# The second pass of Q and K by seven products of halves, x reloaded for the router, and a score bound from sums of squares

## The chip, the cores and the metric

The kernel runs on one core of one Trainium2 chip. The metric is the device time of one launch in microseconds; of several runs the median is given. TensorE (PE) multiplies, VectorE (DVE) and ScalarE (ACT) do elementwise work, GpSimd (POOL) a little of it, and DMA queues move data between memory and the core; SP, ACT and POOL each issue DMAs on a queue of their own.

## The reference

A gate g mixes two branches over one sequence of S = 2048 tokens with D = 1024 features. Branch a is attention with 32 heads of 32. Branch b is a router that picks, for each token and head, one of 8 x 8 experts, with the scores of two small key tables.

```python
g = sigmoid((x * gate_w).sum(-1, keepdims=True))
a = attention(x, wqkv) @ wo                    # H = 32, Dh = 32
b = router(x, w_q, k1, k2, u, v)               # E = 8, top 1, 32 heads, dk = 128
return g * a + (1 - g) * b
# router: q = x @ w_q; s1 = q1 . k1; s2 = q2 . k2; the best of each gives an expert;
# act = gelu(x . u[expert]); out = sum over heads of act * v[expert]
```

All inputs are float32, normal with a spread of 0.05.

## The kernel before

**Matrix products.** A float32 product is made of three fp32r products: each operand is split into a high part (`hi`, a rounding copy on ACT) and a low part (`lo`, source minus high part on DVE; `split`, L100), and high by high, high by low and low by high are summed in one PSUM bank. There are eight banks of 128 x 512.

**Q and K** are made transposed: 8 chunks of 128 rows each for Q and for K (two chunks `(w, c)` for each c; w is 0 for Q, 1 for K), and 4 token blocks n of 512. x lies in SBUF as split blocks `x_blk[n, ki]`, ki being the half of the features; only four places (names `xh0` to `xl3`) of that size exist beside scratch, so two passes are made.

**First pass**, token blocks 2 and 3. Chunk 0 is made while x comes in (L420), chunk 1 by four plain blocks of 24 matmuls (L514). Chunks 2 to 7 are six *units* (`qk_unit`, L519): Q and K of one chunk number by the two token blocks by the two halves of features is a 2 x 2 by 2 x 2 block product, and it is made by seven products P1 to P7 of 12 matmuls (`Halves.product`, L156) in place of eight. The left operands A11, A12, A22 and S1 to S4 are weights or sums of weights; the right ones are blocks of x or the sums T1 to T4 of blocks, made once for a pass. Each unit makes the next unit's left operands, and puts its products together on DVE (`u2`, `u3`, `u5`, `c1`; `tt`, L162; the copy of P1 is ACT's, L532). `hooks` names further work after a product of a unit.

**Second pass**, token blocks 0 and 1: 32 plain blocks of 24 matmuls (L734), in the order of `chunks`, weights split into two places (`pairs`) ahead (`w_chunk`). `between[b]` names further work after block b:

- `folds`: 32 times w_q is folded with the keys into the router's weights, 8 matmuls each (`fold`, L332) into a bank; every fourth fold ends with ACT's copy of the bank (`wt`), four transposes on PE (`fold_t`, L353), a copy and a store to DRAM (`WPD`) on POOL's queue;
- `gate`: DVE multiplies blocks of x by the gate's column and adds them up (`zacc`, L665); the high and low parts of each block are taken one after the other; `gate_sums` (L680) sums over partitions on PE;
- blocks of x are loaded again and split (`again`): (3,0) and (2,1), so that all four token blocks lie split in SBUF when the router starts;
- `load_wp`, `split_wp`: the router's weights, 8 pieces of 128 x 448 (the folded part, from DRAM, into six buffers `wpr`) and 128 x 64 (`ugr`), are loaded and split beside the last four blocks (`between[28]` to `[31]`).

Every block of Q and K goes out by `evac`: ACT writes the high part (L241), DVE the low part (L254) and then the largest magnitude of the block's rows (L248, `amax4`); both parts are stored to DRAM on ACT's queue (qdh, qdl, kdh, kdl).

**Router** (L781, L864 on): 16 tiles of 128 tokens, 24 matmuls each, then steps on DVE and POOL. At tile 4 `bound` multiplies the largest magnitudes of Q and K, row by row, and sums them over a head's 32 rows; the largest sum decides at run time whether a general branch with a shift of the scores runs after the fast path (`general`, at the end).

**After it** follow values and experts, attention, and the output projection. Instructions of an engine run in the order of the program; loads are issued by SP in program order too, and a load waits until its place is free.

Of the kernel before, what the change touches and what calls it, by code (L numbers as in the profile page):

```python
# [17 lines left out]
S = 2048  # L18
# [14 lines left out]
def gated_mha_peer_kernel(ctx, tc, xT, wqkv, wv, wo, wq, k12, ug, v, out):  # L33
# [23 lines left out]
    ZD = dram.tile([1, S], F32, name="zd")  # L57
    SMD = [dram.tile([4, S], F32, name=f"smd{g}") for g in range(G)]
# [11 lines left out]
    cbits = const.tile([1, 1], F32, name="cbits")  # L70

# [6 lines left out]
    const.tile([128, 120], F32, name="fill")  # L78
# [123 lines left out]
    amax = const.tile([128, 2, KC], F32, name="amax")  # L202
    amax4 = const.tile([128, 2, KC, NQ], F32, name="amax4")
# [7 lines left out]
    wb.tile([128, 512], F32, name="s1")  # L211
# [7 lines left out]
    def load_w(which, c, pieces=((0, KC),), queue=nc.sync, single=False):  # L219
        i = 0 if single else w_no[0] % 3  # L220
        w_no[0] += 1
        t = (wb if i else wa).tile([128, KC, 128], F32, name=f"wraw{i}")
# [21 lines left out]
    maxima = []  # L244

    def evac_max():
        for args in maxima:
            nc.vector.tensor_reduce(*args, axis=AX.X, op=OP.max, apply_absolute_value=True)  # L248
        maxima.clear()

    def evac_lo(later=False):
# [3 lines left out]
        maxima.append((amax4[:, which, c, n:n + 1], hi.bitcast(F32)))  # L255
        if not later:
            evac_max()
# [43 lines left out]
    slots = [wqp.tile([128, 4, 512], F32, name="wqt")]  # L301

# [12 lines left out]
    def load_wq(n):  # L315
        slot = slots[0 if n < 3 or 11 <= n < 15 else (n - 2) % 3 if n < 15 else (n - 14) % 3]
# [66 lines left out]
    def split_x(n, kc):  # L383
        ki, k = divmod(kc, HC)
        t = x_blk[n, ki]
        split(t[:, 0, k], t[:, 1, k], raws[ki][:, k, (n - 2) * 512:(n - 1) * 512])
# [36 lines left out]
    hq = Halves(lambda name: wb.tile([128, 512], F32, name="s1"), bank,  # L423
# [27 lines left out]
    second = {(0, 0): "A12", (0, 1): "A22", (1, 0): "S3", (1, 1): "S2"}  # L451

    def split_w1(w, *kis):
        for ki in kis:
            t = w_parts[w, ki] = op_places[second[w, ki]]
            split(t[:, 0], t[:, 1], wraw[w, 1][:, ki * HC:(ki + 1) * HC])
# [37 lines left out]
    split_w1(0, 0, 1)  # L494
    split_w1(1, 0)
    for name, place in (("T1", "xl0"), ("T3", "xh0")):
# [3 lines left out]
    split_w1(1, 1)  # L500
# [6 lines left out]
             [(hq.parts, "S3"), (hq.parts, "S2"), (combine, "T4", "xh3"), (hq.parts, "A22"), (folds, (1,), (2,))]]  # L507
    for w in range(2):
        for n in (2, 3):
            ps = bank()  # L510
            for kc in range(KC):
                for a, b, first, last in ((0, 0, kc == 0, False), (0, 1, False, False),
                                          (1, 0, False, kc == KC - 1)):
                    nc.tensor.matmul(ps, w_parts[w, kc // HC][:, a, kc % HC], x_at(b, n, kc), start=first, stop=last)  # L514
            evac(w, 1, n, ps)
            for f, *args in steps[2 * w + n - 2]:
                f(*args)

    def qk_unit(c, order, nxt, hooks):  # L519


        p, done = {}, set()
        k0 = 3 if c == 2 else 0
        for k, name in enumerate(order):
            if nxt and k == k0:
# [9 lines left out]
            if name == "P2" and "P6" not in p:  # L535
# [4 lines left out]
                evac_hi(0, c, 2, u5)  # L540
                evac_lo()
            if nxt and k == k0:
# [3 lines left out]
                if c + 2 <= KC:  # L546
                    load_w(0, (c + 2) % KC)
            if name == "P6":
# [6 lines left out]
                evac_hi(1, c, 3, u5)  # L555
            if "P6" in p:
                for q, (o, w, n) in (("P2", (c1, 0, 2)), ("P3", (u2, 0, 3)), ("P4", (u3, 1, 2))):
                    if q in p and (q, 0) not in done:
# [3 lines left out]
                        evac_lo(later=not nxt and q != "P2")  # L562
# [1323 lines left out]
```

## Time and profile before

| | us |
|---|---|
| median of 3 runs (1788.53 to 1789.68) | 1789.48 |
| the profiled execution | 1789.42 |
| its span, first to last instruction | 1787.6 |
| first pass of Q and K | 0 to 180 |
| second pass | 180 to 378 |
| router | 378 to 465 |
| values and experts | 465 to 625 |
| attention | 625 to 1563 |
| output projection | 1563 to 1788 |

The page's first part gives busy time and share of the span of each engine, the second the same in 40 slices:

```profile
PE 1776.9 (99%) x14663; PEld 1007.2 (56%) x14663; DVE 1502.5 (84%) x1319; ACT 1216.3 (68%) x1612; POOL 295.7 (17%) x357
...
PE   9999999999999999999999999999999999999998
...
DVE  6868776258886869999999999999999989998885
ACT  4434422221233399999999999999999999993221
```

A slice is 44.7 us, so slices 1 to 4 are the first pass, 5 to 8 the second, 9 and 10 the router. DVE and ACT have idle time in all of these, least where a 7 or 8 stands; PE has none.

### The profile page before, as it was taken

The numbers are of one execution on the slowest core, as the hardware profiler recorded it, in microseconds if no ns is written. First come the engines' busy times: TensorE is split into PE (matmuls) and PEld (weight loads), VectorE is DVE, ScalarE is ACT, GpSimd is POOL, SyncE is SP. The second block draws the span as 40 slices with busy tenths as digits, with TensorE's granted clock in tenths as the row PEclk, the third lists the DMA queues.
The fourth block names the chain that finished last, engine by engine and source line by source line (L and its number), as shares of the span: only waits on it lengthen the run. The fifth ranks groups of instructions, "written<-read, shape, count | busy, mean of one in ns | idle before, by whom it ended". The sixth has DMA issues, their size and how long they took to land.

```text
span 1787.6 us, 35584 instructions
## 1 busy us (share of the span) xinstructions
PE 1776.9 (99%) x14663; PEld 1007.2 (56%) x14663; DVE 1502.5 (84%) x1319; ACT 1216.3 (68%) x1612; POOL 295.7 (17%) x357
## 2 busy tenths in 40 slices
PE   9999999999999999999999999999999999999998
PEld 7877777788888843333333333333343333337887
DVE  6868776258886869999999999999999989998885
ACT  4434422221233399999999999999999999993221
POOL 0222000026501201111112121121111121221000
PEclk9999999999999999999999999999999999999999
DMA  7898988831227788779889888797898898978331
GB/s 237 246 287 248 271 268 283 280 117 67 77 101 255 268 201 167 168 162 196 187 182 209 183 192 196 173 192 167 186 208 189 189 203 186 208 156 277 122 104 70
DMA packets 138428, 343.16 MB, mean 192 GB/s; under 512 B 17452, under 2 KB 50560, under 8 KB 119940
## 3 DMA queue, kind: packets, MB, share of 16 engines
q0 software_dynamic: 24080, 139.27, 38.1%
q1 hardware_dynamic: 94020, 165.64, 28.9%
q10 hardware_dynamic: 20160, 35.92, 7.0%
q8 instruction: 116, 1.90, 0.4%
q14 instruction: 52, 0.43, 0.1%
HBM read 151.47 MB, written 86.09 MB: 133 GB/s over the span
## 4 chain that ended last, share of the span: by engine, by line
PE 95%; DVE 2%; ACT 1%; issue 1%; DMA 1%; SPq 0%; DVEq 0%; ACTq 0%
PE o L1282 27%; PE ring L296 25%; PE bk L156 13%; PE bk L734 10%; PE pa L156 7%; PE bk L781 5%; PE bk L900 2%; PE bk L332 2%; PE bk L420 1%; PE bk L514 1%; ACT P L1154 1%; DVE acc L1321 1%; PE pa L1553 1%; DMA smd<-ssb 0%; DMA xh<-in_xT 0%
## 5 line engine op out<-in xcount | busy, mean ns | idle before, releaser
L1154 ACT ACTIVATE P<-ring 128x512 f32<-128x512 f32 (+2 forms) x980 | 792.0, 942 | 3.3 <-PE ring L296 1.8
L1321 DVE TENSOR_TENSOR acc<-acc,P 128x2048 f32<-128x2048 f32 x199 | 455.3, 2291 | 36.9 <-ACT P L1154 23.1
L1282 PE MATMUL o<-P,V 128*32 128x512 f32 (+2 forms) x3992 | 449.3, 534 | 0.3 <-ACT P L1154 0.3
L296 PE MATMUL ring<-z,k 32*128 32x512 f32 x4224 | 345.3, 425 | 0.0
L296 PEld LDWEIGHTS ring<-z,k 32*128 32x128 f32 x4224 | 179.4, 183 | 265.1 <-ACT P L1154 200.5
L1321 DVE TENSOR_TENSOR rb<-rb,P 128x2048 f32<-128x2048 f32 x89 | 203.9, 2291 | 15.7 <-ACT P L1154 9.6
L1282 PEld LDWEIGHTS o<-P,V 128*32 128x32 f32 x3992 | 92.5, 108 | 186.5 <-issue 163.0
L296 PE MATMUL ring<-z,z 32*128 32x512 f32 x1908 | 156.4, 425 | 0.5 <-ACT P L1154 0.5
L296 PEld LDWEIGHTS ring<-z,z 32*128 32x128 f32 x1908 | 81.7, 183 | 112.8 <-ACT P L1154 76.3
L1311 POOL DMA_DIRECT2D P<-P x70 | 65.7, 939 | 376.7 <-ACT P L1154 376.7
L1154 ACT ACTIVATE wo_raw<-ring 128x512 f32<-128x512 f32 (+2 forms) x126 | 107.1, 943 | 0.0
L241 ACT ACTIVATE hi<-bk 128x512 fp32r<-128x512 f32 x40 | 23.7, 595 | 119.1 <-PE bk L734 100.8
L734 PE MATMUL bk<-xh,e 128*128 128x512 f32 x384 | 94.2, 394 | 0.0
L734 PE MATMUL bk<-xl,e 128*128 128x512 f32 x384 | 92.3, 389 | 0.0
L254 DVE TENSOR_TENSOR lo<-bk,hi 128x512 fp32r<-128x512 f32 x40 | 27.6, 689 | 68.8 <-ACT hi L241 67.3
L734 PEld LDWEIGHTS bk<-xh,e 128*128 128x128 f32 x384 | 71.0, 188 | 22.0 <-issue 3.4
L734 PEld LDWEIGHTS bk<-xl,e 128*128 128x128 f32 x384 | 72.1, 188 | 15.0
L1321 DVE TENSOR_TENSOR acc<-acc,wo_raw 128x2048 f32<-128x2048 f32 x32 | 73.3, 2292 | 4.6 <-ACT wo_raw L1154 1.4
L1154 ACT ACTIVATE vhl<-ring 128x512 f32<-128x512 f32 (+2 forms) x90 | 76.2, 923 | 0.0
L102 DVE TENSOR_TENSOR e<-wraw,e 128x512 fp32r<-128x512 f32 (+3 forms) x64 | 54.8, 865 | 23.3 <-ACT e L101 22.7
L156 PE MATMUL pa<-woh,acc 128*128 128x512 f32 x224 | 72.5, 389 | 0.0
L1329 POOL DMA_DIRECT2D acc<-acc x41 | 32.8, 800 | 227.5 <-DVE acc L1321 123.4
(302 smaller groups left out, 2485.0 us busy)
## 6 DMA issues: line engine op xcount, KB each, us to landing
P<-P POOLq DMA_DIRECT2D x70, 1024.0 KB, 9.9
wqt<-in_wq SPq DMA_DIRECT2D x26, 1024.0 KB, 6.6
wraw<-in_wqkv SPq DMA_DIRECT2D x30, 512.0 KB, 6.1
acc<-acc POOLq DMA_DIRECT2D x21, 512.0 KB, 8.4
qdh<-hi ACTq DMA_DIRECT2D x32, 256.0 KB, 5.5
qdl<-lo ACTq DMA_DIRECT2D x32, 256.0 KB, 5.6
kdh<-hi ACTq DMA_DIRECT2D x32, 256.0 KB, 2.5
kdl<-lo ACTq DMA_DIRECT2D x32, 256.0 KB, 5.7
```

The costliest lines, as they stand in the source:

```text
L102: (on or nc.vector).tensor_tensor(out=lo, in0=src, in1=hi.bitcast(F32), op=OP.subtract)
L156: nc.tensor.matmul(ps, self.a[a][i][:, k, :], self.b[b][j][k], start=(not first and k == 0 and i == j == 0), stop=(k == HC - 1 and i == 1))
L296: yield j, nc.tensor.matmul(ps, a[rows], b[rows], start=(i == 0), stop=(i == 2))
L332: nc.tensor.matmul(ps[32 * quad:32 * quad + 32, :], kpad[:, quad % 2, i, :], t[:, quad, :], start=(i == 0), stop=(i == 3))
L734: nc.tensor.matmul(ps, t[:, kc // HC, a, kc % HC], x_at(b, n, kc), start=first, stop=last)
L781: nc.tensor.matmul(ps, x_at(a, t // 4, kc)[:, tok], b, start=first, stop=last)
L900: nc.tensor.matmul(p, x_at(a, t // 4, kc)[:, tok], b, start=first, stop=last)
L1154: return nc.scalar.activation(to, ps, AF.Exp, scale=SCALE, bias=-SHIFT_LIMIT)
L1282: nc.tensor.matmul(O[h][32 * j:32 * j + 32, c0:c1], Vt[g][:, kt, 32 * j:32 * j + 32], p[:, j * 512 + c0:j * 512 + c1], start=(kt == 0), st ...
L1311: nc.gpsimd.dma_start(P[h, b], P[h, a], accum_op=OP.add)
L1321: nc.vector.tensor_add(out, a, b)
L1329: nc.gpsimd.dma_start(ACC[h][:n], ACC[h][n:2 * n], accum_op=OP.add)
```

## The change

The second pass now works like the first. `NB` holds the pass's first token block. The eight blocks of chunks 0 and 1 stay plain (`plain_block`), and the sums T1 to T4 and the operands of unit 2 are made beside them; chunks 2 to 7 are units of seven products. The places that T1 to T4 take are wanted from x, so blocks of x are loaded again later: (2,1) and (1,0) in unit 7 (`load_spare`, `from_spare`), and (2,0), (3,0), (3,1) between the router's tiles (`more_x`). The gate's products are spread over first-pass units, plain blocks, unit 3 and the router; a block's piece `z` is stored to DRAM (`ZPD`) and read back for `gate_sums` after router tile 8.

```diff
+    hooks[6]["P1"] += [(load_raws, 0, "xl3")]
+    hooks[7]["P1"] += [(load_raws, 1, "xh2"), (load_w, 0, 1), (split_w, 0, 0, 0, "A11")]
...
+    for c, (n, ki) in ((3, (3, 1)), (4, (2, 0)), (5, (2, 1))):
+        for q, part in (("P7", 0), ("P2", 1)):
+            hooks[c][q] += [(gate_part, n, ki, part, c < 5 and part == 0)]
...
+    NB[0] = 0
...
     evac_lo()
+    plain_block(0, 0, 0, [(gate_raw, 1, 0, True), (x_sum_, "T1"), (folds, [12], [13])])
+    plain_block(1, 0, 0, [(combine, "T1", "xl2"), (x_sum_, "T3"), (split_w, 0, 1, 0, "A12"), (split_w, 0, 1, 1, "S4"),
+                          (load_w, 1, 2)])
+    w_parts[0, 0], w_parts[0, 1] = op_places["A11"], op_places["S3"]
+    plain_block(0, 0, 1, [(combine, "T3", "xh3"), (gate_raw, 1, 1), (gate_store, 1), (folds, [13], [14])])
+    plain_block(1, 0, 1, [(x_sum_, "T2"), (split_w, 1, 1, 0, "A22"), (split_w, 1, 1, 1, "S2"), (load_w, 0, 3)])
+    w_parts[0, 0], w_parts[0, 1] = op_places["A12"], op_places["S4"]
+    plain_block(0, 1, 0, [(combine, "T2", "xl3"), (set_rows, 2), (operands, "S3", "S1", "A11", "S2"),
+                          (folds, [14], [15])])
+    plain_block(0, 1, 1, [(gate_raw, 0, 1, True), (hq.parts, "A12"), (operands, "S4"), (hq.parts, "S4")])
+    plain_block(1, 1, 0, [(hq.parts, "S3"), (hq.parts, "S1"), (x_sum_, "T4"), (folds, [15], [16])])
+    plain_block(1, 1, 1, [(hq.parts, "S2"), (hq.parts, "A22"), (combine, "T4", "xh1"), (load_w, 1, 3), (fold_t,)])
...
+    hooks[2]["P1"] += [(to_spare, "xh2"), (load_wq, 17), (load_wq, 18)]
+    for i in range(5):
+        ns = range(16 + 3 * i, 19 + 3 * i)
+        hooks[2 + i]["P6"] += [(folds, ns, [n + 3 for n in ns if n + 3 < 32])]
+        if i:
+            hooks[2 + i]["P2"] += [(fold_t,)]
+    hooks[3]["P7"] += [(gate_part, 0, 0, 0)]
+    hooks[3]["P2"] += [(gate_part, 0, 0, 1), (gate_store, 0)]
+    hooks[6]["P6"] += [(load_spare,)]
+    hooks[7]["P1"] += [(wr.close,), (folds, [31])]
+    hooks[7]["P7"] += [(fold_t,), (open_router,)]
+    hooks[7]["P5"] += [(split_wp, 0), (split_wp, 1)]
+    hooks[7]["P6"] += [(from_spare, 2, 1, "xl3"), (split_wp, 2)]
+    hooks[7]["P4"] += [(from_spare, 1, 0, "xh1")]
+    hooks[7]["P2"] += [(split_wp, 3), (split_wp, 4)]
+    for c in range(2, KC):
+        qk_unit(c, ORDER2 if c == 2 else ("P1", "P7", "P5", "P6", "P4", "P2", "P3") if c == KC - 1 else ORDER,
+                c + 1 if c < KC - 1 else None, hooks[c])
...
+    for kc in range(5, KC):
+        split_wp(kc)
...
+    more_x = {1: [(from_spare, 2, 0, "xh2"), (load_xr, 3, 1, 0)],
+              3: [(lambda: gate(0, xr[3, 0]),), (gate_store, 3), (from_spare, 3, 0, "xh3"), (load_zacc,)],
+              6: [(from_spare, 3, 1, "xl2")], 8: [(gate_sums,)]}
```

The 32 blocks of the second pass, `between` and `w_chunk` go. `open_router` opens three buffers `wpr` and places for the first five split weights; the last three get theirs when the pass is over, and are split behind it.

The bound on the scores no longer takes maxima. ACT squares each block and sums its rows (`accum_out`), an entry of `squares` being issued with the next product or evacuation; `bound` sums the largest of these over a head's rows, for Q and for K, multiplies the two sums (Cauchy-Schwarz), and compares with the square of the limit.

```diff
-    def evac_max():
-        for args in maxima:
-            nc.vector.tensor_reduce(*args, axis=AX.X, op=OP.max, apply_absolute_value=True)
-        maxima.clear()
+    def evac_sq():
+        for acc, src in squares:
+            nc.scalar.activation(src, src, AF.Square, accum_out=acc)
+        squares.clear()
...
-        nc.tensor.matmul(pb2[:1, :H], ones[:, 0:1], prf, start=True, stop=True)
-        nc.vector.tensor_reduce(cbits, pb2[:1, :H], axis=AX.X, op=OP.max)
+        nc.tensor.matmul(pb2[:1, :2 * H], ones[:, 0:1], sqf, start=True, stop=True)
+        nc.vector.tensor_copy(kq, pb2[:1, :H])
+        nc.vector.tensor_mul(kq, kq, pb2[:1, H:2 * H])
+        nc.vector.tensor_reduce(cbits, kq, axis=AX.X, op=OP.max)
...
-        with tc.If(creg[0] > int(np.float32(SHIFT_LIMIT / SCALE).view(np.int32))):
+        with tc.If(creg[0] > int(np.float32((SHIFT_LIMIT / SCALE) ** 2).view(np.int32))):
```

How it moves instructions shows at three places. The first is DVE at the start of the second pass (`lo<-bk`: the low part of a block; `e_140`, `e_154`: places of split weights; `amax_136`: the maxima; `xl_1310`: the raw block of x that is loaded for this pass). Before:

```order
L254 TENSOR_TENSOR lo<-bk_1593,hi 128x512
L248 TENSOR_REDUCE amax_136<-hi 128x1
L254 TENSOR_TENSOR lo<-bk_1623,hi 128x512
L248 TENSOR_REDUCE amax_136<-hi 128x1
L102 TENSOR_TENSOR e_140<-wraw_1432,e_140 128x2x512
L254 TENSOR_TENSOR lo<-bk_1655,hi 128x512
L248 TENSOR_REDUCE amax_136<-hi 128x1
L254 TENSOR_TENSOR lo<-bk_1694,hi 128x512
```

After, in the new program's line numbers (L620 and L622 are the gate's products, L446 a sum T, L104 a low part of `split`, L260 the low part of a block):

```order
L260 TENSOR_TENSOR lo<-bk_1619,hi 128x512
L620 TENSOR_SCALAR z<-xl_1310,gw 128x512
L622 SCALAR_TENSOR_TENSOR z<-xl_1310,gw,z 128x512 x3
L446 TENSOR_TENSOR xl_1310<-xl_1310 128x4x512
L260 TENSOR_TENSOR lo<-bk_1662,hi 128x512
L104 TENSOR_TENSOR xl_1694<-xl_1310,xl_1694 128x2048
L446 TENSOR_TENSOR xl_1310<-xh_1466,xl_1310 128x4x512
L104 TENSOR_TENSOR e_154<-wraw_1469,e_154 128x512 x2
```

The low parts of the blocks stood close together, with a maximum behind each; now gate products, sums T1 and T3 and their low part stand between them, and the split of Q's weights of chunk 1 (`e_154`, the operand `A12` and beside it `S4`) behind these.

The second place is PE at the end of the second pass. Before (`bk_` are banks, `xh_`, `xl_` the blocks of x; L781 is the router's first tile, whose weights are `wph`, `wpl`):

```order
L353 MATMUL bk_2773<-ident,wt 128x128 x4
L734 MATMUL bk_2781<-xh_1451,e_140 128x512 x12
L734 MATMUL bk_2781<-xl_1468,e_140 128x512 x12
L734 MATMUL bk_2852<-xh_1523,e_140 128x512 x12
L734 MATMUL bk_2852<-xl_1547,e_140 128x512 x12
L734 MATMUL bk_2892<-xh_1451,e_141 128x512 x12
L734 MATMUL bk_2892<-xl_1468,e_141 128x512 x12
L734 MATMUL bk_2932<-xh_1523,e_141 128x512 x12
L734 MATMUL bk_2932<-xl_1547,e_141 128x512 x12
L781 MATMUL bk_3011<-wph_2824,xh_1451 128x512
```

After (L158 are the products, here P1, P7, P5, P6, P4, P2, P3 of unit 7; L338 is the last fold, L359 its transposes; L814 is the router's first tile):

```order
L158 MATMUL bk_2856<-xh_1493,e_143 128x512 x12
L338 MATMUL bk_2769<-wqt,kpad 32x512 x4
L158 MATMUL bk_2882<-xh_1736,e_143 128x512 x12
L359 MATMUL bk_2895<-ident,wt 128x128 x4
L158 MATMUL bk_2931<-xl_1694,e_144 128x512 x12
L158 MATMUL bk_2956<-xl_1820,e_144 128x512 x12
L158 MATMUL bk_2988<-xh_1955,e_154 128x512 x12
L158 MATMUL bk_3012<-xl_1519,e_154 128x512 x12
L158 MATMUL bk_3045<-xl_1591,e_154 128x512 x12
L814 MATMUL bk_3135<-wph_2907,xh_1493 128x512
```

The last fold and its transposes moved to six products before the router's first tile, where eight half blocks of plain work stood behind the transposes.

The third place is DVE where the router's weights are split. Before (`wpl`: a split weight's low part, in a folded part of 448 columns and one of 64):

```order
L254 TENSOR_TENSOR lo<-bk_2781,hi 128x512
L248 TENSOR_REDUCE amax_136<-hi 128x1
L102 TENSOR_TENSOR wpl_2825<-wpr,wph_2824 128x448
L102 TENSOR_TENSOR wpl_2825<-ugr,wph_2824 128x64
L102 TENSOR_TENSOR wpl_2827<-wpr,wph_2826 128x448
L102 TENSOR_TENSOR wpl_2827<-ugr,wph_2826 128x64
L254 TENSOR_TENSOR lo<-bk_2852,hi 128x512
L248 TENSOR_REDUCE amax_136<-hi 128x1
```

After (L164 puts a unit's products together, `u` and `c`; `xl_2979` is the reloaded block (2,1) of x):

```order
L104 TENSOR_TENSOR wpl_2908<-wpr_2925,wph_2907 128x448
L104 TENSOR_TENSOR wpl_2908<-ugr,wph_2907 128x64
L104 TENSOR_TENSOR wpl_2910<-wpr_2927,wph_2909 128x448
L104 TENSOR_TENSOR wpl_2910<-ugr,wph_2909 128x64
L164 TENSOR_TENSOR u_2969<-c_2869,bk_2956 128x512
L164 TENSOR_TENSOR u_2970<-u_2969,bk_2882 128x512
L164 TENSOR_TENSOR u_2969<-u_2969,bk_2931 128x512
L164 TENSOR_TENSOR u_2971<-u_2970,bk_2931 128x512
L164 TENSOR_TENSOR xl_2979<-xh_2783,xl_2979 128x2048
L104 TENSOR_TENSOR wpl_2912<-wpr_2929,wph_2911 128x448
L104 TENSOR_TENSOR wpl_2912<-ugr,wph_2911 128x64
L164 TENSOR_TENSOR u_2970<-u_2970,bk_2988 128x512
```

The splits stood between the evacuations of plain blocks; the recombination of unit 7 and a reloaded block of x stand between them now, and the splits behind the second stand behind these.

More of the change, by code (lines that the diff above doesn't have):

```diff
@@ L448, in t_tile, with split_w @@
         return xp.tile([128, 2, HC, 512], F32R, name=place)
[L451 to L456, printed above, removed]
+    def split_w(w, c, ki, name):
+        t = w_parts[w, ki] = op_places[name]
+        split(t[:, 0], t[:, 1], wraw[w, c][:, ki * HC:(ki + 1) * HC])
     def combine(name, place):
@@ L699, in split_wp @@
+        for kc in range(3):
+            load_wp(kc)
     def split_wp(kc):
```

321 lines of the change are left out of this document (160 added, 161 removed).

## The prediction, made before the changed kernel ran

> **What bounds the kernel now.** I read four views in this order: the page's head, the chain of waits, the busy time by stretch, and the timeline where one stage hands over to the next.
>
> ```profile
> span 1787.6 us, 35584 instructions
> PE 95%; DVE 2%; ACT 1%; issue 1%; DMA 1%; SPq 0%; DVEq 0%; ACTq 0%
> ...
> 54.00:180.00 126.00, 126.00 (x598) 97.80 (x599) 98.37 (x129) 47.96 (x77) 30.46 (x23) 1.00 0.85 265
> 0.00:180.00 180.00, 177.72 (x822) 138.57 (x823) 138.78 (x192) 74.09 (x118) 30.90 (x28) 1.00 0.82 256
> 180.00:378.00 198.00, 198.00 (x958) 150.02 (x957) 117.29 (x162) 53.96 (x78) 3.83 (x5) 1.00 0.82 261
> 378.00:465.00 87.00, 87.00 (x386) 71.74 (x385) 68.91 (x144) 12.61 (x24) 48.43 (x54) 1.00 0.19 61
> ```
>
> TensorE is 95% of the chain. The last four rows give, after a stretch and its length, the busy time of PE, of its weight loads, of DVE, ACT and POOL, the granted clock, and the DMA share. They are chunks 2 to 7 of the first pass of Q and K, that whole pass, the second pass, and the router. In the second pass PE is busy for all of its 198.00 us and DVE for 117.29, ACT for 53.96. So a matmul taken out there shortens the kernel, as long as nothing else makes PE wait. The profiled execution took 1789.42 us, 1.8 more than its span; the median of the runs is 1789.48. I make the sum against 1789.42. A measurement of this kernel can tell about 0.2%, 3.6 us, from no change.
>
> **What the change removes.** Here is the chain of waits (start, length, engine, line and count) at the end of the first pass, which already works by seven products, and through the second pass:
>
> ```profile
> 157.42 11.12 PE bk L156 x48
> 168.54 0.44 PE bk L353 x4
> 168.98 10.93 PE bk L156 x48
> 179.91 21.76 PE bk L734 x96
> 201.67 0.99 PE bk L332 x8
> ...
> 267.80 2.71 PE bk L332 x24
> ...
> 306.84 1.00 PE bk L680 x8
> ...
> 356.01 21.81 PE bk L734 x96
> 377.83 27.20 PE bk L781 x120
> ```
>
> A plain block is 24 matmuls: 21.76 / 4 = 5.44 us. A product of halves is 12: 10.93 / 4 = 2.73 us. The second pass had 32 blocks, 768 matmuls. Now chunks 0 and 1 keep 8 plain blocks (192), and chunks 2 to 7 take 6 x 7 products of 12 (504), 696 in all. 72 matmuls at 21.76 / 96 = 0.2267 us are **16.3 us less**. The 20 folds of the router's weights (L332; 0.99 us for one, 2.71 for three) stay: five triples and five singles now, five triples, a pair and three singles before, 0.1 us more. The row sums of the gate (1.00 us at L680) move into the router and cost the same there.
>
> **Work that only changes engine.** These are groups of instructions, with count, busy sum and mean in ns:
>
> ```profile
> L248 DVE TENSOR_REDUCE amax<-hi 128x1 f32<-128x512 f32 x64 | 43.1, 675 | 0.0
> ...
> L1154 ACT ACTIVATE P<-ring 128x512 f32<-128x512 f32 x566 | 341.1, 637 | 3.3 <-PE ring L296 1.8 <-DMA P<-P 1.0 <-DVE acc L1321 0.4
> L254 DVE TENSOR_TENSOR lo<-bk,hi 128x512 fp32r<-128x512 f32 x40 | 27.6, 689 | 68.8 <-ACT hi L241 67.3 <-DMA qdl<-lo 1.5
> L241 ACT ACTIVATE hi<-bk 128x512 fp32r<-128x512 f32 x40 | 23.7, 595 | 119.1 <-PE bk L734 100.8 <-DMA qdh<-hi 6.3 <-DMA kdl<-lo 4.8
> L162 DVE TENSOR_TENSOR u<-u,bk 128x512 f32<-128x512 f32 x29 | 19.4, 681 | 0.4
> L665 DVE SCALAR_TENSOR_TENSOR zacc<-xl,ugr,zacc 128x512 f32<-128x512 f32 x24 | 18.0, 750 | 0.6
> L101 ACT ACTIVATE wph<-wpr 128x448 fp32r<-128x448 f32 x8 | 4.6, 570 | 3.1 <-DVE lo L254 2.5 <-ACT hi L241 0.6
> L102 DVE TENSOR_TENSOR wpl<-wpr,wph 128x448 fp32r<-128x448 f32 x8 | 5.0, 619 | 1.0 <-ACT wph L101 1.0
> L162 DVE TENSOR_TENSOR xl<-xl,xl 128x2048 fp32r<-128x2048 f32 x2 | 4.6, 2284 | 0.0
> L598 ACT ACTIVATE xl<-xl 128x2048 fp32r<-128x2048 f32 x2 | 3.8, 1902 | 0.0
> ```
>
> DVE loses the 64 maxima, 43.1 us. ACT gains 64 squares with a sum. The trace shows none; a copy of the same shape takes 0.595, an exponential 0.637, and I take 0.6: 38 us, about 0.6 us per 2.7 us of PE. ACT had 128 us busy of 378 in the two passes, so this hides, except where ACT is late already. In first-pass units 3 to 5 the gate adds two times four products of 0.75, 6.0 us, against four maxima (2.7 us) that go. DVE was busy 98.37 of the 126.00 us of the six units, 16.4 of 21; 19.7 with 3.3 more still fits: **0**, since operands are made a unit ahead. If that cover failed, a unit would lose the 3.3 us that DVE gains. The first units (2 to 7) of the second pass then resemble the first pass, without a gap: **0**. The router gains three blocks of x (2.28 each) and four gate products (3.0): 68.91 + 9.9 = 78.8 us of DVE in 87. It fits, with eight PSUM banks as slack: 0, up to 1.5.
>
> **First loss: the plain blocks at the start of the second pass.** Beside the 8 blocks (43.5 us) DVE now makes four differences of x and their low parts (8 x 2.28), eight evacuations, 12 gate products and some 15 operand pieces; that is about 44 us, so it runs behind. The fifth block (Q of chunk 1) needs `A12`, which comes late in this order.
>
> ```profile
> 190.80 0.69 DVE L254 TENSOR_TENSOR lo<-u,hi 128x512 fp32r<-128x512 f32 x1
> ```
>
> That row is DVE's last piece of the first pass before its maxima: 191.5 us. From there come, before `A12` is ready: an evacuation (0.69), four gate products (3.0), the difference T1 (2.28), an evacuation (0.69), a wait for ACT's copy of T1 (1.90 less 0.69), T1's low part and the difference T3 (4.56), `A12`'s low part (0.68): 13.1 us, so 204.6. PE gets there at 179.9 + 4 x 5.44 + 2 folds of 1.00, and needs the part at its third matmul, 204.1. With the squares and the split of weights in between, ACT's copies in the last first-pass unit come up to 4 us later than before; so the stall is 0 to 4.5 us. If it is 0, DVE still reaches the end of T4's low part (31 us of work and 1.5 of waits later) at about 237, and only then may SP load two fold weights into the same place:
>
> ```profile
> xl<-in_wq SPq DMA_DIRECT2D x6, 1024.0 KB, 6.7
> ```
>
> They land at 243.5 to 249; the folds 17 and 18 stand behind six products of unit 2, at 245 to 246. So one stall or the other, 0 to 6.5 together. I take **3**, near the first row's end with half of ACT's delay.
>
> **Second loss: the end of the second pass.** Before, the last blocks were plain and the router's weights were split beside them. Now unit 7's last recombination, two blocks of x and eight splits stand in one line on DVE, and the router's first tile waits for all eight splits. The copy of the folded weights comes late too:
>
> ```profile
> 168.74 0.58 ACT L532 ACTIVATE c<-bk 128x512 f32<-128x512 f32 x1
> 168.87 0.69 DVE L102 TENSOR_TENSOR e<-wraw,e 128x512 fp32r<-128x512 f32 x1
> ...
> 363.91 0.22 DVE L102 TENSOR_TENSOR wpl<-ugr,wph 128x64 fp32r<-128x64 f32 x1
> ```
>
> The first row is ACT's copy of P1 in unit 7 of the first pass. P1 ended on PE at 157.42 + 2 x 2.73 = 162.9, so ACT was 5.8 us late. In the second pass the copy of the fold (`wt`) comes right behind this one, and PE wants to transpose it after one more product, 3.7 us after P1. Without four maxima and with two squares I put `wt` at about 5.2: PE waits 1.5 us. From the end of P6, DVE does: seven recombinations (0.68) and four low parts (0.68), 7.5; two blocks of x, 4.6; six splits at 0.62 + 0.22, 5.0; three small ones, 0.7: 17.8 us. It also waits for ACT: 2.5 before the first block of x (a copy of 0.6, then 1.90), 1.9 before the second, 0.7 before the split 3, 2.0 at the end (two squares and the stores' issue): 7.1. So the last split is ready 24.9 us after P6. PE needs 3 x 2.73 + 5.44 = 13.6 us for what follows P6 up to the tile's end. That is a stall of 11.3, and with the 1.5 it is 12.8; the sum may be 10 if the waits are half as long, and more if loads are late (below). I take **12.5**.
>
> **Sum.** -16.3 + 0.1 + 3 + 12.5 = -0.7 us: 1789.42 - 0.7 = 1788.7, predicted **1789 us**, no change that a measurement can tell. The chain ahead of the router gives back what the matmuls save. After the router nothing moves but the start.
>
> **A rule on the clock.** All stretches quoted show a granted clock of 1.00, and the trace has no pause of PE between 10 and 1560 us longer than a fraction of a us, so no row shows what a pause of 6 us does. The Trainium skill, "TensorE: Matmul & The Clock Gate", section "What's actually happening", says that a window of about 3.4 us without work sets the clock to half until about as long a busy time has passed. By that page a long stall would cost 1.7 us more, an estimate from its window. By rows, as a mechanism: if the tile behind the stall ran at half pace, its 5.44 us would be up to 10.9, and half of it 2.7 more.
>
> **The rivals.**
>
> 1. *The seam is shorter (faster).* DVE starts its line at P6's end, the `wt` copy is in time, block 5 has its operand: losses of 11 only, -16.3 + 0.1 + 11 = -5.2: **1784**. For it: DVE has 43 us less. Against it: the lag of 5.8 us and the 17.8 us of work in one line.
> 2. *A load holds the line (slower).* ACT and DVE have the first two splits ahead of P6's recombination in their queues; behind the waiting split stand all of unit 7's evacuations and x. If the load lands late, everything moves by as much.
>
> ```profile
> wpr<-wpd SPq DMA_DIRECT2D x8, 224.0 KB, 11.1
> kdh<-hi ACTq DMA_DIRECT2D x32, 256.0 KB, 2.5
> ```
>
> The loads are issued when unit 7's operands are done, about 4 us after P1, and P6 ends 9.6 us after P1. So this decides from a landing time of about 5 us on. With the measured 11.1 us and 1.5 us for two splits they end at 16.6, 7 us after P6 against 1.5: 5.5 us more, **1794**. Against it: 11.1 us was behind 3 MB of other loads; now at most 2 MB stand ahead, and a like size took 2.5 us.
> 3. *The clock drops behind the stalls:* 2.7 us more, **1791.5**, inside the range of no change.
> 4. *The bound is looser and sends the kernel into the general branch.* The inputs have a spread of 0.05, so a Q or K value has a variance of 0.05^4 x 1024 = 0.0064, and the sum over 512 tokens and 32 rows is 105. 105 x 105 = 11,000 against a limit of (30 x 5.66)^2 = 28,800: excluded.
>
> **Numbers.** Forecast 0.46, rival 1 0.29, rival 2 0.19, rival 3 0.06. The forecast's own range is 1786 to 1793. The whole range goes from rival 1 with its waits 2 us shorter, 1782, to rival 2 with the late stall at the plain blocks in full, 1796. Faster than 1785.8 is rival 1, with little from the forecast's edge: 0.29; slower than 1793.1 is rival 2 with some of rival 3: 0.22; the same 0.49.
>
> **What would show it.** In the profile after: 696 matmuls in the second pass, 72 fewer; PE idle before the fifth plain block, on DVE's `e`; PE idle in the router's first tile on `wpl`, 9 to 13 us; the last `wpl` 23 to 26 us behind P6. Wrong if the router's first tile waits under 5 us, if the plain blocks lose over 7, or if PE loses time within units 3 to 6 or in the router behind its first tile, which I hold to be covered.

## The result, and the profile after

The changed kernel takes **1837.6 us** (1835.4 to 1838.6, 6 runs) against 1789.6: a ratio of 1.0267, with a 95% interval of 1.0254 to 1.0280. The prediction was 1789, no change, with a range of 1782 to 1796. It was wrong by 48.6 us. The head of the page after (that of before stands ahead of the prediction; the last line gives each engine's share of the chain):

```profile
span 1836.3 us, 35735 instructions
PE 1785.0 (97%) x14591; PEld 1005.8 (55%) x14591; DVE 1539.8 (84%) x1340; ACT 1283.5 (70%) x1787; POOL 327.7 (18%) x377
...
PE   9979979999999999999999999999999999999998
...
PEclk9989989998999999999999999999999999999999
...
PE 82%; DVE 7%; issue 4%; DMA 3%; ACT 2%; POOL 1%; SPq 0%; ACTq 0%; DVEq 0%; POOLq 0%
```

PE runs 14591 instructions, 72 fewer, as the change says. But the span less PE's busy time, 10.7 us before, is 51.3 now: **40.6 us of waits**. And PE's busy time rose by 8.1 us although 16.3 us of matmuls are gone, so what is left ran **24.4 us slower**. 40.6 + 24.4 - 16.3 = 48.7 us, the difference of the spans. The digits of PEclk show where: the first two 8s stand at the slices in which PE's own row has a 7, the third at the slice right behind the router's start (413 to 459 us). Not all of the 24.4 us are the clock's. PE's busy time in pieces of 1 us, times the share of the clock that was not granted in each, adds up to 19.5 us, and to nothing before. Of the other 5, 1.7 lie ahead of the first unit (53.3 us of PE busy there against 51.5).

The busy times by stretch show the same by stage (columns as in the prediction):

```profile
56.00:203.43 147.43, 131.41 (x597) 100.17 (x598) 99.01 (x128) 62.01 (x123) 31.51 (x23) 0.95 0.70 233
203.43:268.82 65.39, 54.10 (x230) 38.90 (x228) 50.91 (x54) 28.32 (x49) 0.00 (x0) 0.90 0.64 200
268.82:408.00 139.18, 134.98 (x652) 101.19 (x650) 83.93 (x112) 61.54 (x126) 31.47 (x25) 0.98 0.79 266
408.00:431.06 23.06, 15.88 (x49) 11.45 (x48) 14.09 (x45) 9.63 (x23) 2.03 (x2) 0.70 0.68 213
```

The rows are the units of the first pass, the plain blocks, the units of the second pass, and the router's first two tiles. The clock in the last column but two is under 1.00 in each. What PE waited for up to 600 us (total, times, longest):

```profile
PE bk L158 <- DVE u L164: 11.6, 2, 8.5
PE bk L814 <- ACT wph L103: 7.2, 2, 5.4
PE bk L359 <- ACT wt L342: 6.7, 4, 4.2
PE bk L338 <- DMA wqt<-in_wq: 6.2, 2, 5.9
PE bk L517 <- DVE e L104: 3.9, 1, 3.9
```

Between the points where stages begin on PE:

| stage (us) | before | after | predicted | measured |
|---|---|---|---|---|
| to the first unit | 53.8 | 55.9 | 0 | +2.1 |
| units of the first pass | 125.9 | 147.5 | 0 | +21.6 |
| second pass (65.4 plain, 139.2 units) | 197.9 | 204.6 | -14.2 | +6.7 |
| router | 87.4 | 101.8 | +13.5 | +14.4 |
| values and experts | 162.0 | 166.4 | 0 | +4.4 |
| the rest | 1160.5 | 1160.0 | 0 | -0.5 |

The first row is scatter: it lay between 52.8 and 56.7 us in the runs below.

The largest piece, in the first pass, can be followed. Here is SP's queue before (start, duration of the issues, transfer, count; a gap ahead of a row is a wait):

```profile
90.55 0.33 SPq L83 DMA_DIRECT2D wqt<-in_wq  x1
91.41 1.19 SPq L83 DMA_DIRECT2D xl<-in_wq  x2
102.56 2.29 SPq L83 DMA_DIRECT2D wraw<-in_wqkv  x2
```

and after, with the rows of POOL and PE that follow:

```profile
103.81 0.33 SPq L85 DMA_DIRECT2D zpd<-z  x1
104.24 0.37 SPq L85 DMA_DIRECT2D wqt<-in_wq  x1
104.71 0.89 SPq L85 DMA_DIRECT2D xl<-in_wq  x2
113.68 3.41 SPq L85 DMA_DIRECT2D wraw<-in_wqkv  x2
...
121.97 1.27 POOL L140 TENSOR_TENSOR s<-wraw,wraw 128x512 f32<-128x512 f32 x1 [20.31 <-DMA wraw<-in_wqkv]
...
130.97 8.21 PE L158 MATMUL bk<-xh,e 128*128 128x512 f32 x24 [8.45 <-DVE u L164]
```

The store of the gate's piece (`zpd<-z`) stands on SP's queue until DVE has finished z. Three loads of fold weights, 3 MB, stand behind it and go out 12 us later than before, counted from the first unit, and the weights of Q and K behind these. POOL makes its sums from the weights 8 us after their issue; DVE's split waits for the sum and ends at 125.1 us; four gate products (3.8 us) and a second split stand behind it, and only then the recombination `u`, at 129.4; and PE waits 8.45 us for the bank that `u` frees. So the late loads and the gate's products meet in this wait. The 24 matmuls behind it take 8.21 us, where 24 in a row took 5.60 before: half the clock for a while.

### The profile page after: what moved, and what is told of

It reads as the page before. It is cut to its first block, busy times and chain, and to the rows that moved or that the text cites. A ratio compares the mean times of both kernels' runs of the same rounds, so it can differ in the third digit from the quotient of the medians.

```text
span 1836.3 us, 35735 instructions
## 1 busy us (share of the span) xinstructions
PE 1785.0 (97%) x14591; PEld 1005.8 (55%) x14591; DVE 1539.8 (84%) x1340; ACT 1283.5 (70%) x1787; POOL 327.7 (18%) x377
## 4 chain that ended last, share of the span: by engine, by line
PE 82%; DVE 7%; issue 4%; DMA 3%; ACT 2%; POOL 1%; SPq 0%; ACTq 0%; DVEq 0%; POOLq 0%
PE o L1328 27%; PE ring L301 24%; PE bk L158 13%; PE pa L158 7%; PE bk L814 3%; PE bk L517 3%; PE bk L426 1%; PE pa L1592 1%; PE bk L338 1%; DVE u L164 1%; ACT P L1200 1%; DMA xh<-in_xT 1%; POOL eq L828 1%; PE pa L1599 1%; DVE z L622 1%
## 5 line engine op out<-in xcount | busy, mean ns | idle before, releaser
L158 PE MATMUL bk<-xh,e 128*128 128x512 f32 x504 | 124.0, 402 | 11.6 <-DVE u L164 11.6
L158 PE MATMUL bk<-xl,e 128*128 128x512 f32 x504 | 121.8, 396 | 0.0
L158 PEld LDWEIGHTS bk<-xh,e 128*128 128x128 f32 x504 | 96.6, 194 | 38.5 <-issue 16.5
L104 DVE TENSOR_TENSOR e<-wraw,e 128x512 fp32r<-128x512 f32 (+2 forms) x92 | 65.9, 726 | 50.8 <-ACT e L103 50.5
L158 PEld LDWEIGHTS bk<-xl,e 128*128 128x128 f32 x504 | 95.6, 191 | 23.2 <-issue 3.4
L246 ACT ACTIVATE hi<-u 128x512 fp32r<-128x512 f32 x36 | 22.8, 632 | 97.2 <-DVE u L164 89.8
L158 PE MATMUL pa<-woh,acc 128*128 128x512 f32 x224 | 72.5, 389 | 0.0
L103 ACT ACTIVATE e<-wraw 128x512 fp32r<-128x512 f32 (+2 forms) x92 | 54.5, 601 | 16.9 <-DVE wraw L140 6.3
## 6 DMA issues: line engine op xcount, KB each, us to landing
P<-P POOLq DMA_DIRECT2D x70, 1024.0 KB, 10.8
xh<-in_wq SPq DMA_DIRECT2D x10, 1024.0 KB, 10.9
```

Source lines behind the costliest of these rows:

```text
L103: nc.scalar.activation(hi, src, AF.Copy)
L104: (on or nc.vector).tensor_tensor(out=lo, in0=src, in1=hi.bitcast(F32), op=OP.subtract)
L158: nc.tensor.matmul(ps, self.a[a][i][:, k, :], self.b[b][j][k], start=(not first and k == 0 and i == j == 0), stop=(k == HC - 1 and i == 1))
L246: nc.scalar.activation(hi, src, AF.Copy)
```

## The experiments

**Whether the store holds SP's queue.** Only the queue of the stores is changed:

```diff
-        dma(ZPD[:, n * 512:(n + 1) * 512], z)
+        dma(ZPD[:, n * 512:(n + 1) * 512], z, nc.gpsimd)
```

> The changed kernel with the stores of the gate's pieces (zpd<-z) issued by POOL instead of SP; nothing else. Theory Q (SP's queue): each store waits on SP for DVE's last gate product, and the loads of fold weights, of Q/K weights and of x behind it go out late. Then the waits of PE in the first-pass units (8.45 and 3.12 us) and of the fold in the plain blocks (5.92 us) go, with the half-clock time behind each (about 2 to 2.5 us): the first pass ends at about 183 to 186 instead of 203.4, the whole is about 25 to 30 us shorter, 1807 to 1813. Theory W (the gate's products themselves fill DVE's line): the waits stay, and the time is within 3 us of 1837.6.

It took 1815.7 us, a ratio of 1.0151 to the kernel before, with an interval of 1.0134 to 1.0168 (both are given in brackets from here on): 21.8 less than the changed kernel. The waits of 8.45, 3.12 and 5.92 us are gone (0.5 of the last is left); the plain blocks take 57.4 us, not 65.4. But the first pass fell only to 136.0. Waits for the fold's copy of up to 3.4 us stay in its units.

**The gate's work in the first pass left out** (an empty tuple in the loop over (3,1), (2,0), (2,1); zeros are stored):

> The changed kernel without the gate's work in the first pass: the products of blocks (3,1), (2,0), (2,1) and their two stores on SP are left out, zeros stand for them. Theory Q: the first pass ends where it ends with the stores on POOL, within 2 us, 181 to 186; the plain blocks still wait for the fold's load, so the time is about 1812 to 1818. Theory W: the first pass ends at about 181 to 183 here, while with the stores on POOL it stays above 200.

1813.6 us (1.0131, 1.0114 to 1.0148); the units of the first pass take 125.9, to 0.1 us what they took before, with no wait. So of the 21.6 us, 11.5 came from the queue and 10.1 from the gate's products themselves: neither theory alone.

**The same products one at a time** (and the stores on POOL):

```diff
-        for q, part in (("P7", 0), ("P2", 1)):
-            hooks[c][q] += [(gate_part, n, ki, part, c < 5 and part == 0)]
...
+    turns = [(c, q) for c in range(3, 7) for q in ORDER]
...
+            c, q = turns.pop(0)
+            hooks[c][q] += [(gate_one, n, *one_, i == 0)]
```

> As the kernel with the stores on POOL, and the gate's products of blocks (3,1), (2,0), (2,1) and (0,0) are issued one at a time behind a product of PE (7 to a unit), not in lumps of four. DVE's work is the same. Theory lump (a lump of 3 to 4 us stands ahead of a recombination, ACT's copies wait for that, and the fold's copy wt behind them): the 7.4 us of waits in the first-pass units and the 4.4 us in unit 3 of the second pass go, with about 2 us of half clock for each of the longer ones; first pass at 181 to 183 instead of 190.8, total 1815.7 less 12 to 17: 1799 to 1804. Theory load of DVE (its sum of work counts): first pass stays at 188 or more, total 1811 to 1816.

1809.6 us (1.0109, 1.0092 to 1.0126), 6 less than with the stores moved; the first pass takes 128.5. Of the 10.1 us, 7.5 came from the lumps. How a lump holds PE shows in the run before it, with the stores on POOL: DVE's four products, the recombination, ACT's copy of the fold, and the transposes that wait for that:

```profile
125.85 4.02 DVE L622 SCALAR_TENSOR_TENSOR z<-xh,gw,z 128x512 f32<-128x512 f32 x4
...
129.78 0.68 DVE L164 TENSOR_TENSOR u<-u,bk 128x512 f32<-128x512 f32 x1
...
131.55 0.58 ACT L342 ACTIVATE wt<-bk 128x512 f32<-128x512 f32 x1
...
132.18 0.66 PE L359 MATMUL bk<-ident,wt 128*128 128x128 f32 x4 [3.43 <-ACT wt L342]
```

The whole fell short of the forecast, since the plain blocks took 61.5 us instead of 57.4, and a wait of 3.1 us (4.4 with the lump) stays in unit 3.

**The plain blocks.** A12 and S4 split right behind the first block:

> As the kernel with spread products, and Q's weights of chunk 1 (A12, S4) are split right behind the first plain block, ahead of the gate's products, the sums T1 and T3 and their parts. Theory order (the fifth block waits only because A12 stands late in DVE's line): its waits of 0.7 and 3.9 us and the half clock behind go, 5 to 9 us less. Theory load of DVE (the plain blocks carry more DVE work than PE work): the wait moves to what now stands later, T1's or T3's part or the fold, 0 to 3 us less.

1809.5 us (1.0105, 1.0089 to 1.0122), no less. PE's rows of that run:

```profile
226.20 0.61 PE L517 MATMUL bk<-xh,e 128*128 128x512 f32 x2
230.59 1.65 PE L517 MATMUL bk<-xh,e 128*128 128x512 f32 x3 [3.77 <-DVE e L104]
```

The fifth block no longer waits; the seventh does, for K's weights, as long. On DVE four gate products (3.11 us) and the sum T2 (2.28) stand ahead of them. Next, with spread products, the gate's 8 products from raw (1,1) and (0,1) taken out of the plain blocks and put singly, as 16 (high and low parts apart), into units 2 to 5:

> As the kernel with spread products, and the gate's products of blocks (1,1) and (0,1), 8 from raw blocks between the plain blocks, are taken out there and issued one at a time (16, from high and low parts) in units 2 to 5 of the second pass. Theory DVE in the plain blocks (some 45 us of PE work carry as much DVE work, so whatever stands last waits): the 3.9 us wait for a weight's low part and the 1.0 us of the fold shrink to under 2 together, with the half clock behind them: plain blocks 52 to 55 us instead of 61.5, total 1800 to 1804. Theory order or load (one late operand, whatever DVE has to do): 60 or more, total 1808 to 1812.

1818.2 us (1.0155, 1.0140 to 1.0171), 8.6 **more**; the plain blocks stay at 61.0, since what A12 waits behind is still there, and unit 3 now has this:

```profile
293.90 1.12 PE L359 MATMUL bk<-ident,wt 128*128 128x128 f32 x4 [10.60 <-ACT wt L342]
```

Both edits together, and the products in units 3 to 6:

> As the kernel with A12 early, and the gate's 8 products from raw blocks (1,1) and (0,1) are taken out of the plain blocks and issued singly (24 of them are in all) from the fifth product of unit 3 to the end of unit 6 of the second pass. Neither edit alone shortened the plain blocks (60.7 and 61.0 us against 61.5). Theory order (each edit alone only hands the wait on: A12 early to the K weights behind the gate, the gate gone to A12 behind T1 and T3): both together remove the 3.8 us wait with its half clock, plain blocks 53 to 56 us, total 1800 to 1805. Theory sum (DVE's whole work of these blocks is too much): 59 or more, total 1806 to 1810. In unit 3 the wait for the fold's copy should be 3 us as with spread products, since no product of the gate is in unit 2 or at the start of unit 3.

1812.9 us (1.0126, 1.0109 to 1.0143). The plain blocks take 58.4 us: the 3.8 us wait shrinks to 0.8, a fold's load is waited for by 2.9 instead, and a unit later on waits 5.0 for the fold's copy. The time can't be told from that with A12 early alone. Then three loads of fold weights moved behind the weights of Q and K:

```diff
-        hooks[2 + i]["P6"] += [(folds, ns, [n + 3 for n in ns if n + 3 < 32])]
...
+        hooks[2 + i]["P3" if i == 1 else "P6"] += [(folds, ns, nxt if i else [])]
+        if i == 0:
+            hooks[3]["P1"] += [(folds, [], nxt)]
...
```

> As the kernel before it, and the three loads of fold weights (3 MB) that go out at the end of unit 2 of the second pass go out one product later, behind the weights of Q and K that unit 3 waits for; unit 3's folds move two products back with them. Theory load (the fold's copy wt waits on ACT behind operands that wait for POOL's sums, and these for K's weights, which queue behind 3 MB): the wait of 3 to 4 us in unit 3 goes, units 132 to 135 us instead of about 137, 3 to 5 us less. Theory ACT (the copy is late for ACT's and DVE's own work): no change, within 1.5 us.

1810.7 us (1.0116, 1.0099 to 1.0133), which the intervals can't tell from the run before. The units take 140.8 us, as there, with a wait of 4.3 us for a fold's copy at another place. What holds it there was not settled by this.

**The gate left out of both passes**, then squares, then both:

> The changed kernel without the gate's products and stores in both passes (zeros stand for them; the router's own piece stays). Theory gate (what the second pass loses before the router is the gate's work in DVE's line and its stores): the plain blocks take 50 to 53 us instead of 65, the units behind 132 to 134 instead of 139, and the whole about 1794 to 1799: the 12 us of the router's start and 4 us behind it are left. Theory rest (sums, operands and squares are already too much for these blocks): plain blocks 57 or more, total 1803 or more.

1798.0 us (1.0049, 1.0032 to 1.0065): **39.5 us less than the changed kernel**. The stretches in that run:

```profile
54.04:179.96 125.92, 125.92 (x601) 97.78 (x598) 84.76 (x108) 62.67 (x123) 33.04 (x27) 1.00 0.88 289
179.96:234.51 54.55, 50.77 (x230) 37.73 (x228) 39.89 (x40) 27.96 (x48) 0.00 (x0) 0.97 0.74 207
234.51:368.66 134.15, 132.66 (x651) 99.19 (x649) 77.96 (x104) 61.55 (x126) 31.06 (x25) 1.00 0.82 274
```

DVE has 14 us less to do in the first pass, 11 in the plain blocks, 6 in the units behind; PE loses 21.6, 10.8 and 5.0 us less there.

> The kernel with spread products, without the squares (the sums for the bound are ones). In the kernel before the squares cost nothing. Theory line (where DVE is late, ACT's squares, which wait for DVE's low part of the same block, hold ACT's copies behind them): first pass 126 to 127 us instead of 128.5, unit 3's wait of 3.1 us under 1.5, total 3 to 7 us less than 1809.6. Theory hidden: within 2 us of 1809.6.

Without squares, from the kernel with spread products: 1808.0 us (1.0095, 1.0079 to 1.0112) against 1809.6, within the 2 us of "hidden".

> The changed kernel without the gate's work in the passes and without squares. If both only take time in lines that are late, the passes come near PE's own time: first pass 126, plain blocks 49 to 51, units 131 to 133, total 1790 to 1796: what is left above the kernel before less 16 us is the router's start and the stage behind it.

1800.6 us (1.0059, 1.0043 to 1.0076): no less than with the squares in. The squares don't hold the line.

**The bound alone**, in the kernel before (maxima out, squares in):

> The kernel before, with the score bound alone changed: 64 maxima less on DVE, 64 squares with a sum on ACT. Theory hidden (PE is the bound in both passes and ACT and DVE have idle time): 1788 to 1791, no difference. Theory ACT late (the squares push ACT's copies, on which banks and operands wait): some waits of PE in the units, 1793 or more.

1794.7 us (1.0030, 1.0018 to 1.0042), 5 us more, which looked like a price of the squares. But PE had no wait in either pass. The tiles behind the constants had moved by 32 bytes in this kernel. With the same edit and 8 floats of filling:

> The kernel before with the score bound alone changed, as in the earlier run, but with the fill tile of the constants 8 floats longer, so that all tiles behind it lie at the addresses that they had before. Theory squares (ACT's squares cost the 5 us of that run): 1793 to 1796 again. Theory places (the 5 us lay in attention and projection, where nothing of the bound runs, and came from tiles moved by 32 bytes): 1788 to 1791.

1790.7 us (1.0003, 0.9994 to 1.0013): no difference. The expectation put the 5 us into attention; by the traces 2.6 of them were in the router (90.0 us against 87.4), the rest in pieces of about 1 us or less behind it. The router's largest group before, then in the run with the tiles moved (mean ns of one behind the comma):

```profile
L781 PE MATMUL bk<-wph,xh 128*128 128x512 f32 x128 | 42.1, 390 | 0.0
```

```profile
L781 PE MATMUL bk<-wph,xh 128*128 128x512 f32 x128 | 42.9, 396 | 0.0
```

With the filling it is 42.1 and 390 again, and nothing but places in memory differs between the last two runs. The changed kernel has eight floats more among its constants (`gw`), which make up for the 32 bytes. Its router's matmuls behind the first two tiles take 389 to 394 ns, so about 1 us of this kind, at most, is in its 48.

**The router's start.** Blocks (2,1) and (1,0) split behind tiles 0 and 1, stores on POOL:

```diff
-    hooks[7]["P6"] += [(from_spare, 2, 1, "xl3"), (split_wp, 2)]
-    hooks[7]["P4"] += [(from_spare, 1, 0, "xh1")]
+    hooks[7]["P6"] += [(split_wp, 2)]
...
-    more_x = {1: [(from_spare, 2, 0, "xh2"), (load_xr, 3, 1, 0)],
+    more_x = {0: [(from_spare, 1, 0, "xh1")],
+              1: [(from_spare, 2, 1, "xl3"), (from_spare, 2, 0, "xh2"), (load_xr, 3, 1, 0)],
...
```

> As the kernel with the stores on POOL, and the two reloaded blocks of x that stood in unit 7's end, (2,1) and (1,0), are split in the router instead, behind tiles 0 and 1. Theory line (the router's first tiles wait for one line on DVE and ACT: recombination, x, splits): 4.6 us of DVE and 3.8 us of ACT leave that line, the loss at the router's start (12.2 us in the changed kernel: 7.2 of wait, the rest at a lower clock) falls to 3 to 7, and the time is 5 to 9 us below the kernel with the stores on POOL. Theory load (the splits wait for their three buffers and their loads): the loss stays at 10 or more and the time within 2 us.

1811.5 us (1.0124, 1.0107 to 1.0140), 4.3 less than with the stores moved. Of the two waits 1.6 us are left, and the router takes 92.1 us, not 101.2; but values and experts take 170.1, not 166.4, with a new wait of 2.4 us for ACT's `gate`, behind a router that now ends in arrears. With A12 early, products spread, and the low parts of four blocks of x on POOL:

> As the kernel with A12 early, and blocks (2,1) and (1,0) of x split in the router as in the run on the router's start; the low parts of the four blocks with n over 1 are made by POOL instead of DVE. Theory DVE bound in the router (68.9 us before, 15 more with all blocks): the router's start loses 3 to 5 us instead of 12, and the values' stage no longer starts with DVE in arrears: router to attention 252 to 256 us instead of 262 (both blocks of x in the router on DVE), 12 to 16 us less than with A12 early alone. Theory POOL bound (57 of 100 us busy, a block 5 to 7 us more): 0 to 6 us less.

1811.6 us (1.0119, 1.0102 to 1.0136): no gain over A12 early alone (1809.5). PE waits 10.6 us for the same `gate`. POOL was busy for 81 us of the 136 from the router's start, with both blocks on DVE for 65 of 133; that the router's own steps on POOL came late by that is likely, and wasn't followed further.

**The clock.** In the changed kernel, matmuls that nobody reads fill the waits of the router's first tile:

```diff
+            if t == 0 and kc in (3, 5):
+                for i in range(22 if kc == 3 else 8):
+                    nc.tensor.matmul(fill, x_at(0, 0, 0)[:, tok], Wp[0][0], start=True, stop=True)
```

> The changed kernel with 30 more matmuls on operands that are ready, into a bank that nobody reads, in the router's first tile: 22 ahead of its fourth weight, 8 ahead of its sixth, 6.8 us at full speed, where PE waited 5.4 and 1.8 us. Theory clock (PE's half speed behind a wait comes from the wait): the matmuls behind run at full speed, the first two tiles take 16 to 18 us instead of 23.1, and the time is 4 to 6 us shorter than the changed kernel's 1837.6 although 30 matmuls more are run. Theory operands (the slow matmuls are slow for what they read or for the load of the other engines): the time is the same or up to 3 us longer.

The first two tiles with the filling:

```profile
409.14:429.82 20.68, 18.92 (x80) 14.36 (x78) 14.07 (x45) 9.66 (x23) 1.72 (x2) 1.00 0.60 182
```

They take 20.7 us instead of 23.1, with 30 matmuls more, at a granted clock of 1.00 instead of 0.70. So the matmuls behind these waits were slow for PE's idle time, not for what they read. The 16 to 18 us of the expectation were an error of the sum: 10.9 us of tiles, 6.8 of filling and the 1.7 of waits left are 19.4. The time, 1835.2 us (1.0255, 1.0241 to 1.0269), can't be told from the changed kernel's.

**All together.** Stores, spread products, fewer products in the plain blocks, x in the router; then with A12 early and the loads moved:

> All edits together: stores on POOL, spread products, fewer products in the plain blocks, two blocks of x in the router. If the losses add up, it is the time of the kernel without gate lumps in the plain blocks less the 4.3 us that the router's edit brought: 1795 to 1799, still slower than the kernel before by 0.3 to 0.5%.

> As the kernel before it, and two reloaded blocks of x moved into the router. If the losses add up: 4 us less than the kernel before it, 1792 to 1797, so still no faster than the kernel before the change by more than 0.1%.

1813.2 us (1.0131, 1.0116 to 1.0147) and 1807.8 (1.0096, 1.0080 to 1.0113). The second has the lowest median of those that compute all, 30 us below the changed kernel and 18 above the one before, but its interval overlaps that of spread products alone (1809.6). The losses did not add up as forecast: in the second the plain blocks still take 59.9 us and the units 140.7.

## Why the prediction was wrong, step by step

- **The matmuls, -16.3 us**: right. 72 instructions of PE are gone.
- **"0, since operands are made a unit ahead"**, for the gate's products in first-pass units: this step failed, with 21.6 us. The sum of busy time was right (DVE 99.01 us in these units, 98.37 before: what the gate adds, the maxima took). The cover was not. First, the step's store was not counted as an instruction on SP's queue with loads behind it (11.5 us). Second, four products in a row stand ahead of a recombination, and ACT's copies and PE's transposes behind that one (7.5 us); spread out, the same work costs 2.6. The fallback that was named, 3.3 us for a unit, was too small as well: three units had the gate, 9.9 us against 21.6.
- **The plain blocks, +3**: wrong in size and in kind. They lose about 17 us (65.4 against 48: 8 blocks of 5.44, 4 folds of 1.0, a transposition). The step took 44 us of DVE work; it is 50.9. The wait for `A12` came (3.9 us and 0.5, inside its 0 to 4.5). A fold waited too, 5.9 us, but not one of those that the step named: folds 17 and 18 did not wait. It was one inside the plain blocks, whose load went out behind another store of `z` (with the stores on POOL 0.5 of the wait is left):

```profile
240.94 0.33 SPq L85 DMA_DIRECT2D zpd<-z  x1
241.36 0.38 SPq L85 DMA_DIRECT2D wqt<-in_wq  x1
```

  The rest is a wait of 1.0 us for a low part of x, and lower clock. 10.8 of the 17 us are the gate's, by the run without it.
- **The units of the second pass, 0**: they take 6.5 us more than the 132.7 that the forecast leaves for them (183.7 for the pass less 51 for the plain blocks). 5.0 of it is the gate's, by the run without it; the largest wait is one of 4.2 us in unit 3.
- **The router's start, +12.5**: the line of work was right, and the number partly by luck. 48 matmuls of 0.2267 us are 10.9, and they took 23.1: 12.2 more. The last split was ready 22.7 us behind P6, where 24.9 were forecast, and `wt` was in time, where 1.5 of wait were forecast. PE's waits were 7.2 us, not 12.8 and not the 9 to 13 of the signs, and ended on ACT's `wph`; 5.0 us of half clock, which the sum had at nothing, filled up the rest. The run with two blocks of x moved out of that line supports it: 1.6 us of the waits were left.
- **"After the router nothing moves"**: wrong by 4.4 us. DVE's slack in the router was counted (78.8 us in 87), but not that its end is handed to the next stage: from 477 to 562 us the chain of work runs over DVE and POOL almost alone, where it was PE's before, and ends in a wait of PE for DVE's `xh` (1.4 us). The run with low parts of x on POOL was meant to shorten this, and made it longer (a wait of 10.6 us for `gate`).
- **Squares hidden**: right (1.0003 in the kernel before), though a square took 0.62 us and the reading of its sum 0.19 more, where 0.6 in all was forecast.
- **The clock, as a rival of 2.7 us at one place**: the mechanism was right, its size was off by a factor of seven, because it was priced for one stall: about 19.5 us over all. The Trainium skill, "TensorE: Matmul & The Clock Gate", section "What's actually happening", adds that the window of about 3.4 us runs freely, so that the moment of the change varies. The traces agree that it varies; a wait alone doesn't tell. First the run with stores on POOL, then that without gate and squares:

```profile
132.18 0.66 PE L359 MATMUL bk<-ident,wt 128*128 128x128 f32 x4 [3.43 <-ACT wt L342]
132.59 2.98 PE L158 MATMUL bk<-xh,e 128*128 128x512 f32 x12
```

```profile
207.62 4.14 PE L516 MATMUL bk<-xh,e 128*128 128x512 f32 x10 [2.17 <-DVE e L104]
```

Behind a wait of 3.43 us, 12 matmuls took 2.98 us, full speed; behind one of 2.17, 10 took 4.14, not 2.3 to 2.6.

Without any gate work in the passes the change still loses: in that run the second pass takes 188.7 us, 9.2 less than before, and the router and the stage behind it 17.9 more. What stays open is which of DVE's, ACT's and SP's orders would free the plain blocks and unit 3 with the gate in place: each edit there handed the wait on, and none was the last.

## What to carry to other kernels

When work moves into the shadow of a pipeline that is full, count its store and its place in every queue, not its share of busy time: stores of 256 KB that waited for their data at the head of SP's queue cost 22 us here, and in the first pass DVE's work in lumps of four operations cost nearly four times what it cost one at a time (10.1 us against 2.6). Where TensorE is the bound and has had no pause, put a price on the clock behind new waits too: here it was half of their length, as a mean (19.5 us to 40.6), though one wait of 3.43 us cost nothing. And before a part is blamed for a few us, see that the tiles of the variant lie where they lay.

## What the runs showed of the hardware

- 32 bytes of shift in tile addresses made the router's matmuls slower, 395 to 396 ns on average against 389 to 390, and the kernel by 0.3%; the shift undone, the difference was gone. Why was not tried.
- The half clock outlasts the wait, and a second wait draws it out: in the router's start the first two tiles ran at a mean of 0.70 over 23 us, for waits of 5.4 and 1.8, and full clock came back some 6 us after the second. Around the wait of 8.45 us in the first pass of the changed kernel (clock in the last column but two) it falls while PE is idle, and comes back only some 5 us after the work began again:

```profile
120.00:125.00 5.00, 2.52 (x12) 1.72 (x10) 1.06 (x1) 1.01 (x2) 2.87 (x3) 1.00 1.03 376
125.00:130.00 5.00, 0.00 (x0) 0.00 (x0) 4.89 (x7) 0.68 (x2) 2.12 (x2) 0.61 0.93 393
130.00:135.00 5.00, 4.03 (x10) 3.20 (x11) 3.71 (x7) 1.47 (x3) 0.00 (x0) 0.50 0.07 25
135.00:140.00 5.00, 5.00 (x21) 4.06 (x20) 4.28 (x6) 1.45 (x4) 1.65 (x1) 0.87 0.35 105
```
